# Reordering the first head's loads and keeping TensorE busy in its last waits: one decode kernel, two small edits

## The chip, the core and the metric

The kernel runs on one core of a Trainium2 chip. The metric is the device time of one execution in microseconds. A profile's span is about 2 us shorter than the timed run that it belongs to (1275.8 against 1277.7 for the kernel before). In the lines of the profile, PE is TensorE, PEld its weight loads, DVE VectorE, ACT ScalarE, POOL GpSimd, and SPq the queue that SyncE fills. The *granted clock* is the share of TensorE's full clock, here 1.00 or 0.50.

## The reference, cut to what matters

One token attends to a long cache, and a small gated block is added:

```python
xn = _layernorm(x)                                   # x: 1 x 1 x 448
q  = (xn @ wq) as 16 query heads of 256
scores = einsum(q, k_cache) * 256**-0.5              # 8 key heads, 65536 keys of 256, bf16
o  = einsum(softmax(scores), v_cache)
out = x + o @ wo + (xn + gated block of xn)          # the gated block uses w_r, w_gate, w_up, w_down
```

The key and value caches are 268 MB each, and each byte is used once. So 549 MB must be read from memory, and little else costs anything.

## The kernel before

The 65536 keys of a head are 512 columns of 128 partitions, cut into four *units* of 128 columns (8 MiB). Keys use slots 0 and 1 of an on-chip ring in turn, and values use slot 2. All loads go through one queue, in the order in which SyncE issues them. An issue waits until the slot has been read (`FREE`, `FREEH` for half of it, `VFREE`). A unit in `HALVED` is loaded as two halves with two waits.

```python
HALVED = (0, 2, 3, 4)
def k_item(u):
    need = [("FREE", u - 2)] if u >= 2 else ()
    if u >= 2 and u in HALVED:
        need = {0: [("FREEH", u - 2)], 1: need}
    slot_item("k", u, u % 2, ...two halves if u in HALVED..., need)

def v_item(t):
    slot_item("v", t, 2, None, [("VFREE", t - 1)] if t else [("QT",), ("R",), ("CONST",)])

item("wq", ...)
for u in range(U - 1):     # U = 4: key units 0, 1, 2
    k_item(u)
v_item(0)
k_item(U - 1)              # key unit 3
k_item(U)
k_item(U + 1)
for t in range(1, NT):
    v_item(t)
    ...                    # one key unit after each value unit
...                        # the last head, with other weights between
slot_item("v", NT + 3, 2, ...six pieces of LAST = [64, 32, 16, 8, 4, 4] columns..., [("SUM",)])
...                        # last rows of the output weights
```

TensorE transposes the keys (`ps_t`), multiplies them with the query (`ps_q`), and multiplies the values with the probabilities (`ps_o`). After the last value piece come a few tiny matmuls with the output weights, one copy, and the store:

```python
values(NT + 2)
values(NT + 3)             # pe_V: for each piece, wait for its load, then its matmuls
dve_ob(T); pe_oT(T)
...
for k, (i, f0, f1) in enumerate(ENDS):
    W_item("pe", ("wo_end", k))       # the last three loads of output weights
    ...                               # a pair of matmuls, 224 columns each, per block
O("dve", "RESULT", ...tensor_copy...) # then the store
```

Of the kernel before, what the change touches and what calls it, by code (L numbers as in the profile page):

```python
# [14 lines left out]
LAST = [64, 32, 16, 8, 4, 4]  # L15
DIRECT = 2
NF = 2
ACT_M = (3,)
TORD = (3, 0, 1, 2)


def bass_parallel_sum__gqa_block_cached__moe_arch_mod__decode_kernel(
# [21 lines left out]
    _, Hkv, Sk, Dh = A_k_cache.shape  # L44
# [3 lines left out]
    rep = Hq // Hkv  # L48
# [14 lines left out]
    U = NPP // SBN  # L63
    NT = U * (Hkv - 1)
# [21 lines left out]
    def S_(name, shape, dtype):  # L86
        t = nc.sbuf_tensor(name, shape, dtype)
        sb.append(t)
        return t.__enter__()
# [4 lines left out]
    slots = [ring[:, i * SLOT:(i + 1) * SLOT] for i in range(NSLOT)]  # L94
# [18 lines left out]
    p_sb = S_("p_sb", [P, HC, CH, rep], BF16)  # L113
# [25 lines left out]
    sum_f = kt_all[0:1, 3 * KB:3 * KB + 2 * D].bitcast(FP32)  # L139
    DQ = D // NF  # L140
    FROWS = 32 * (NF - 1) + 1
    res_bf = kt_all[:, 3 * KB + 2 * D:3 * KB + 2 * D + DQ]
# [17 lines left out]
    ps_tf = [t[:, :].bitcast(FP32) for t in ps_t]  # L160
# [41 lines left out]
    def put(e, kind, key, fn, sem):  # L202
        if ghost[0] and e == "pe":
            prog[e].append(("g" + kind, lab(e), key, fn, sem))
        elif not ghost[0]:
            prog[e].append((kind, lab(e), key, fn, sem))

    def W(e, *key):
        put(e, "w", key, None, None)
# [3 lines left out]
    def O(e, key, fn, sem=None, n=1):  # L213
        key = key if isinstance(key, tuple) else (key,)
        if not ghost[0]:
            weight[key] = n
        put(e, "o", key, fn, sem or e)

    def alias(e, *key, sem=None):
        put(e, "a", key, None, sem or e)  # L220
# [21 lines left out]
    def item(key, parts, need=()):  # L242
        for n in need:
            W("sp", *n)
        for ap, src, sem in parts:
            semtot[sem] = semtot.get(sem, 0) + 16
            items[key] = (sem, semtot[sem])
            prog["sp"].append(("d", here[0], ("DMA", key, len(prog["sp"])), (ap, src), sem))
# [6 lines left out]
    def slot_item(kd, u, s, parts=None, need=()):  # L255

        o = 0
        for k, (sem, J) in enumerate(parts or [("slot%d" % s, SBN)]):
            ap = slots[s][:, o * Dh:(o + J) * Dh]
            item((kd, u, k), [(ap.rearrange("p (j d) -> p j d", d=Dh), rows_src(kd, u, o, J), sem)],  # L260
                 need[k] if isinstance(need, dict) else need if k == 0 else ())
            o += J
        fed[(kd, u)] = (s, parts or [("slot%d" % s, SBN)])

    def flat_src(src, n):
        return src.rearrange("a b -> (a b)").rearrange("(p n) -> p n", p=P)
# [14 lines left out]
# [4 lines that stand above are left out]
        slot_item("k", u, u % 2, [("slot%d" % (u % 2), CH), ("half%d" % (u % 2), CH)] if u in HALVED else None, need)  # L285

    def v_item(t):
        slot_item("v", t, 2, None, [("VFREE", t - 1)] if t else [("QT",), ("R",), ("CONST",)])

    item("wq", [(wq_area, flat_src(A_wq, WQN), "wq")])  # L290
    for u in range(U - 1):
        k_item(u)
    v_item(0)
    k_item(U - 1)
    k_item(U)
    k_item(U + 1)
    for t in range(1, NT):
# [16 lines left out]
    for g, e in enumerate(("sp", "act")):  # L314
        late.append((e, g))
    items["out"] = ("out", 16 * NF)

    def W_item(e, key):
        W(e, "DMA", key)
# [97 lines left out]
    pe = nc.tensor  # L417

    def mm(*a, **k):
        return pe.matmul(*a, **k)  # L420
# [39 lines left out]
    def ev_engine(m):  # L460
        return "act" if m in ACT_M else "dve"

# [105 lines left out]
    def act_pc(t, c):  # L568
        W("act", "EXP", t // U, rep - 1)
        W("act", "PVC", t - 1, c)  # L570
        n = ((t + 1) % U) * SBN + c * CH
        O("act", ("PC", t, c), lambda it: nc.scalar.activation(out=p_sb[:, c, :, :], in_=S_sb[:, n:n + CH, :], func=ACTF.Copy), "pc")  # L572
# [14 lines left out]
    def pe_V(t, c, first, last, loose=False):  # L587
        W("pe", "PC", t, c)
        if c == 0 and first:
            W("pe", "OB", t - 1)  # L590
        s, parts = fed[("v", t)]
        e0 = 0
        for k, (_, J) in enumerate(parts):
            o0, e0 = e0, e0 + J
            lo, hi = max(o0, c * CH), min(e0, (c + 1) * CH)
            if lo >= hi:
                continue
            W_item("pe", ("v", t, k))
            direct = k > len(parts) - 1 - DIRECT and len(parts) > 1

            def f(it, lo=lo, hi=hi, direct=direct):
                kv = slots[s].rearrange("p (j d) -> p j d", d=Dh)
                if direct:
                    for j in range(lo, hi):
                        for hf in range(NH):
                            ins = mm(ps_m[0:P, C_OT + hf * rep:C_OT + (hf + 1) * rep],
                                     lhsT=kv[:, j, :].rearrange("p (d f) -> p d f", f=NH)[:, :, hf], rhs=p_sb[:, c, j - c * CH, :],
                                     start=False, stop=False, skip_group_check=True)
                    return ins
                for j in range(lo, hi, 2):  # L610
                    g = j // 2 % NG
                    ins = mm(ps_o[32 * g:32 * g + 2 * rep, :],
                             lhsT=p_sb[:, c, j - c * CH:j - c * CH + 2, :].rearrange("p n i -> p (n i)"), rhs=kv[:, j:j + 2, :],
                             start=(first and j < 2 * NG), stop=(last and j >= SBN - 2 * NG),
                             tile_position=(0, 32 * g), skip_group_check=loose)
                return ins

            O("pe", ("PV", t, c, k), f)
        alias("pe", "PVC", t, c)
        if c == HC - 1:  # L620
            alias("pe", "VFREE", t)
        if (t + 1) % U:
            act_pc(t + 1, c)
# [134 lines left out]
    def turn_K(u):  # L758
        t = u - U
        real = t >= 0  # L760
        v = max(t, 0)
        here[0] = ("B", t) if real else ("A", u)

        def ghostly(f):
            def g():
                with maybe(real):
                    f()
            return g

        at = {(2, 2): ghostly(lambda: pe_m1t(v + U - 1)), (3, 0): ghostly(lambda: pe_bc(v + U - 1)),  # L770
              (SETS - 1, 0): ghostly(lambda: pe_oT(v))}

        def block():
            pe_V(v, 0, True, True)
            pe_tot(v)
            pe_V(v, 1, True, True)
            dve_ob(v)

        k_sets(u, range(0, CSETS), at)
        bar()  # L780
        ghostly(block)()
        bar()
        k_sets(u, range(CSETS, SETS), at)

    def fin(g):
        return ps_s[32 * g:32 * g + 1, 0:DQ]

    def values(t):
        for c in range(HC):
            pe_V(t, c, t == NT, t == NU - 1, True)  # L790

    def ending():
# [32 lines left out]
        def fin_base(it):  # L825
            for g in range(NF):
                ins = mm(fin(g), lhsT=ones_f[0:1, 0:1], rhs=sum_f[:, g * DQ:(g + 1) * DQ], start=True, stop=False,
                         tile_position=(0, 32 * g), skip_group_check=True)
            return ins
# [10 lines left out]
        def fin_x(it):  # L840
            for f in range(FO // 2):
                for g in range(NF):
                    ins = mm(fin(g), lhsT=oT_h[:, FO // 2 + f, HL:HL + 1], rhs=wo_x[:, f * D + g * DQ:f * D + (g + 1) * DQ], start=False, stop=False,
# [5 lines left out]
        for k, (i, f0, f1) in enumerate(ENDS):  # L849
            W_item("pe", ("wo_end", k))  # L850

            def f(it, k=k, i=i, f0=f0, f1=f1):
                wo = wo_view(wo_end)
                for hf in range(f0, f1):
                    for g in range(NF):
                        ins = mm(fin(g), lhsT=oT_sb[:, hf, i:i + 1], rhs=wo[:, i, hf, g * DQ:(g + 1) * DQ], start=False,
# [281 lines left out]
```

## Time and profile before

| | kernel before |
|---|---|
| time | 1277.72 us, median of 3 runs (1277.71 to 1278.37) |
| span of the profiled run | 1275.8 us |
| loads in one queue | 549.03 MB, 99.7% of the span |
| TensorE busy | 75% of the span |
| last load landed (completion marks) | 1273.20 us |
| span end after that landing | 2.56 us |

Of the profile's page, the busy row of the engines and the row on the chain of waits that ended last (share of the span of each engine in it):

```profile
PE 956.0 (75%) x9735; PEld 624.7 (49%) x9735; DVE 570.3 (45%) x1078; ACT 436.2 (34%) x655; POOL 8.0 (1%) x38
DMA 80%; PE 17%; issue 1%; ACT 1%; DVE 1%; SPq 0%; ACTq 0%; DVEq 0%
```

The chain is loads for four fifths. TensorE's part is mostly work on what has just landed. The other lines that matter are in the prediction.

### The profile page before, as it was taken

The numbers are of one execution on the slowest core, as the hardware profiler recorded it, in microseconds if no ns is written. First come the engines' busy times: TensorE is split into PE (matmuls) and PEld (weight loads), VectorE is DVE, ScalarE is ACT, GpSimd is POOL, SyncE is SP. The second block draws the span as 40 slices with busy tenths as digits, with TensorE's granted clock in tenths as the row PEclk, the third lists the DMA queues.
The fourth block names the chain that finished last, engine by engine and source line by source line (L and its number), as shares of the span: only waits on it lengthen the run. The fifth ranks groups of instructions, "written<-read, shape, count | busy, mean of one in ns | idle before, by whom it ended". The sixth has DMA issues, their size and how long they took to land.

```text
span 1275.8 us, 23503 instructions
## 1 busy us (share of the span) xinstructions
PE 956.0 (75%) x9735; PEld 624.7 (49%) x9735; DVE 570.3 (45%) x1078; ACT 436.2 (34%) x655; POOL 8.0 (1%) x38
## 2 busy tenths in 40 slices
PE   3898988778777679767778776787777687677664
PEld 3676655445544455444455454454454454444321
DVE  4566554345444455343454344454444554444310
ACT  2455433244333334323333332343332333332300
POOL 2000000000000000000000000000000000000000
PEclk9899999899888899888898888898888998888886
DMA  9999999999999999999999999999999999999998
GB/s 408 426 429 443 432 436 432 434 432 438 434 429 438 427 440 429 436 436 429 438 432 436 432 434 427 440 432 434 438 427 438 432 436 434 432 432 436 426 431 353
DMA packets 12742, 549.20 MB, mean 430 GB/s; under 512 B 1335, under 2 KB 1978, under 8 KB 3386
## 3 DMA queue, kind: packets, MB, share of 16 engines
q1 hardware_dynamic: 12724, 549.03, 99.7%
q8 instruction: 8, 0.13, 0.0%
q14 instruction: 4, 0.03, 0.0%
q10 hardware_dynamic: 6, 0.00, 0.0%
HBM read 549.03 MB, written 0.00 MB: 430 GB/s over the span
## 4 chain that ended last, share of the span: by engine, by line
DMA 80%; PE 17%; issue 1%; ACT 1%; DVE 1%; SPq 0%; ACTq 0%; DVEq 0%
DMA ring<-in_A_v_cache_dram 68%; PE ps_o L420 12%; DMA ring<-in_A_k_cache_dram 7%; DMA kt_all<-in_A_wo_dram 3%; DMA ring<-in_A_wo_dram 2%; PE ps_t L420 2%; PE ps_q L420 1%; PE ps_m L420 1%; ACT kt_all L481 1%; SPq L910 0%; DVE kt_all L479 0%; ACT S_sb L562 0%; PE ps_s L420 0%; DVE kt_all L712 0%; DVE kt_all L815 0%
## 5 line engine op out<-in xcount | busy, mean ns | idle before, releaser
L420 PE MATMUL ps_t<-ident_f,ring 128*128 128x128 f32 x4096 | 586.6, 285 | 84.5 <-DMA ring<-in_A_k_cache_dram 61.6
L479 DVE COPY kt_all<-ps_t 128x1024 bf16<-128x1024 bf16 x768 | 487.0, 684 | 293.8 <-PE ps_q L420 289.0
L420 PEld LDWEIGHTS ps_t<-ident_f,ring 128*128 128x128 f32 x4096 | 450.2, 143 | 237.2 <-issue 135.2
L481 ACT ACTIVATE kt_all<-ps_t 128x1024 bf16<-128x1024 bf16 x256 | 262.0, 1023 | 508.4 <-PE ps_q L420 508.4
L420 PE MATMUL ps_o<-ring,p_sb 128*4 128x512 bf16 x2044 | 177.1, 508 | 204.6 <-DMA ring<-in_A_v_cache_dram 200.3
L420 PEld LDWEIGHTS ps_o<-ring,p_sb 128*4 128x4 bf16 x2044 | 53.0, 101 | 292.6 <-issue 264.2
L420 PE MATMUL ps_q<-kt_all,q_cur 128*2 128x512 bf16 x2056 | 164.9, 398 | 0.3 <-DVE kt_all L479 0.3
L503 ACT ACTIVATE s<-ps_q 98x512 bf16<-98x512 f32 x257 | 151.6, 590 | 1.3 <-PE ps_q L420 1.3
L585 DVE RECIPROCAL rs<-ps_m 128x4 f32<-128x4 f32 x29 | 5.3, 182 | 272.2 <-PE ps_m L420 272.2
L572 ACT ACTIVATE p_sb<-S_sb 128x128 bf16<-128x128 bf16 x64 | 18.9, 307 | 260.8 <-PE ps_o L420 260.6
L420 PEld LDWEIGHTS ps_s<-sel_bf,s 128*128 128x128 bf16 x1032 | 64.7, 98 | 5.3 <-ACT s L503 1.9
L420 PE MATMUL ps_s<-sel_bf,s 128*128 128x8 bf16 x1032 | 63.7, 167 | 1.3 <-ACT s L503 1.3
L628 DVE CAST ob_sb<-ps_o 100x512 bf16<-100x512 f32 x29 | 20.0, 691 | 89.9 <-PE ps_o L420 89.9
L420 PEld LDWEIGHTS ps_q<-kt_all,q_cur 128*2 128x2 bf16 x2056 | 26.4, 79 | 44.2 <-issue 44.2
L420 PEld LDWEIGHTS ps_m<-rowsum,ones_f 128*128 128x128 f32 x58 | 12.3, 264 | 22.6 <-issue 22.6
L481 ACT ACT_TABLE_LOAD x7 | 9.0, 1283 | 20.8 <-PE ps_q L420 20.8
L532 DVE TENSOR_REDUCE m1p<-S_sb (+1 forms) x33 | 13.9, 422 | 4.4
L420 PE MATMUL ps_m<-rowsum,ones_f 128*128 128x4 f32 x58 | 14.8, 326 | 0.0
L530 DVE CAST S_sb<-ps_s 128x256 f32 (+1 forms) x33 | 13.6, 413 | 1.9 <-PE ps_s L420 1.9
L562 ACT ACTIVATE S_sb<-S_sb,negmax 128x512 bf16<-128x512 bf16 x16 | 13.2, 851 | 3.2 <-DVE negmax L556 3.2
L420 PE MATMUL ps_m<-diag,ones_f 2*128 2x2 f32 x58 | 11.2, 260 | 3.6 <-DVE diag L547 0.6
L420 PEld LDWEIGHTS ps_m<-diag,ones_f 2*128 2x128 f32 x58 | 8.7, 187 | 10.5 <-DVE diag L547 10.5
(93 smaller groups left out, 128.3 us busy)
## 6 DMA issues: line engine op xcount, KB each, us to landing
ring<-in_A_k_cache_dram SPq DMA_DIRECT2D x8, 4096.0 KB, 30.5
ring<-in_A_v_cache_dram SPq DMA_DIRECT2D x1, 4096.0 KB, 27.3
ring<-in_A_wq_dram SPq DMA_DIRECT2D x1, 3584.0 KB, 11.5
ring<-in_A_wo_dram SPq DMA_DIRECT2D x1, 2688.0 KB, 28.7
ring<-in_A_v_cache_dram SPq DMA_DIRECT2D x1, 2048.0 KB, 31.8
ring<-in_B_w_gate_dram SPq DMA_DIRECT2D x1, 1568.0 KB, 16.5
ring<-in_B_w_up_dram SPq DMA_DIRECT2D x1, 1568.0 KB, 19.9
ring<-in_B_w_down_dram SPq DMA_DIRECT2D x1, 1568.0 KB
```

The costliest lines, as they stand in the source:

```text
L420: return pe.matmul(*a, **k)
L479: O(e, ("EV", s, m), lambda it: nc.vector.tensor_copy(out=kt[:, :], in_=tb[:, :]), f"ev{m}")
L481: O(e, ("EV", s, m), lambda it: nc.scalar.activation(out=kt[:, :], in_=tb[:, :], func=ACTF.Copy), f"ev{m}")
L503: O("act", ("EVQ", s), lambda it: nc.scalar.activation(out=s2[s % 2][0:QROWS, :], in_=ps_q[0:QROWS, :], func=ACTF.Copy), "evq")
L530: O("dve", ("SCOPY", u), lambda it: nc.vector.tensor_copy(out=S_sb[:, at(it, SBN), :], in_=ps_sn), "sc")
L532: O("dve", ("SMAX", u), lambda it: nc.vector.tensor_reduce(out=m1p[:, :, at(it, 1)], in_=S_sb[:, at(it, SBN), :].rearrange("p n i -> p i n ...
L562: O("act", ("EXP", h, i), lambda it, i=i: nc.scalar.activation(out=S_sb[:, :, i], in_=S_sb[:, :, i], func=ACTF.Exp, bias=negmax[:, i:i + 1 ...
L572: O("act", ("PC", t, c), lambda it: nc.scalar.activation(out=p_sb[:, c, :, :], in_=S_sb[:, n:n + CH, :], func=ACTF.Copy), "pc")
L585: O("dve", ("RS", t), lambda it: nc.vector.reciprocal(out=rs[:, :, :], in_=ps_m[0:P, C_TOT:C_TOT + NH * rep]))
L628: O("dve", ("OB", t), lambda it: nc.vector.tensor_copy(out=ob_sb[0:OROWS, :], in_=ps_o[0:OROWS, :]))
```

## The change

The intent is twofold. First, in the head all four key units are loaded before the first values, since the values are needed much later and TensorE waited for key unit 3. Second, nine extra matmuls, whose result nobody reads, fill TensorE's waits between the last value pieces, so that its clock stays at full speed for the final matmuls.

```diff
+WARM = {0: (5, 512), 1: (2, 512), 2: (1, 512), 3: (1, 256)}
@@ order of the loads
-    for u in range(U - 1):
+    for u in range(U):
         k_item(u)
     v_item(0)
-    k_item(U - 1)
     k_item(U)
     k_item(U + 1)
@@ pe_V, after the matmuls of piece k
             O("pe", ("PV", t, c, k), f)
+            if t == NT + 3 and k in WARM:
+
+                def keep(it, k=k):
+                    n_, cols = WARM[k]
+                    for _ in range(n_):
+                        ins = mm(ps_tf[3][0:2 * rep, 0:cols], lhsT=p_sb[:, c, 0:2, :]..., rhs=slots[0][:, 0:cols],
+                                 start=True, stop=True, skip_group_check=True)
+                    return ins
+
+                O("pe", ("WARM", k), keep)
```

More of the change, by code (lines that the diff above doesn't have):

```diff
@@ L618, in pe_V @@
             O("pe", ("PV", t, c, k), f)
+            if t == NT + 3 and k in WARM:
+                def keep(it, k=k):
+                    n_, cols = WARM[k]
+                    for _ in range(n_):
+                        ins = mm(ps_tf[3][0:2 * rep, 0:cols], lhsT=p_sb[:, c, 0:2, :].rearrange("p n i -> p (n i)"), rhs=slots[0][:, 0:cols],
+                                 start=True, stop=True, skip_group_check=True)
+                    return ins
+                O("pe", ("WARM", k), keep)
         alias("pe", "PVC", t, c)
```

## The prediction

> **What bounds the kernel now.** I read the page first, then the chain of waits in order of time, then the DMA queue's own timeline for the head, and the timelines and stretches of the last 15 us. Four units of 128 key columns make one head; a unit of keys or of values is 8 MiB (8.39 MB). A halved unit goes as two transfers of 4 MiB.
>
> The page, by slices and by queues:
>
> ```profile
> DMA  9999999999999999999999999999999999999998
> q1 hardware_dynamic: 12724, 549.03, 99.7%
> ```
>
> The transfers fill every slice but the last; one queue carries all 549 MB and occupies the 16 engines 99.7% of the span. TensorE at 75% is not the bound. To see whether the transfers ever pause, I add start and length of the DMA pieces of the chain, which gives landing times:
>
> ```profile
> 2.12 49.74 DMA ring<-in_A_k_cache_dram
> 65.07 35.30 DMA ring<-in_A_k_cache_dram
> 144.17 24.06 DMA ring<-in_A_v_cache_dram
> 172.45 34.47 DMA ring<-in_A_v_cache_dram
> 1065.05 32.00 DMA ring<-in_A_v_cache_dram
> 1103.17 32.58 DMA ring<-in_A_v_cache_dram
> ```
>
> Key unit 1 lands at 51.86, the first half of key unit 3 at 100.37, value unit 1 at 168.23, value unit 2 at 206.92; far later two value units land at 1097.05 and 1135.75. From 51.86 to 100.37 the queue moved 20 MiB (both halves of key unit 2, value unit 0, half of unit 3): 48.51 / 5 = 9.70 us per 4 MiB. From 100.37 to 168.23 it moved 28 MiB: 67.86 / 7 = 9.69. Each later pair of units takes 38.69 to 38.70 us, or 9.67 per 4 MiB, which is 433.5 GB/s. So in the head, exactly where the change reorders the queue, there is no pause now: 0.03 us per 4 MiB over twelve pieces is 0.3 us in all. Whatever the order, the same bytes must land, and the kernel's end is the last landing plus a short tail.
>
> The queue's own timeline in the head, and TensorE's one wait there:
>
> ```profile
> 48.34 0.36 SPq L910 DMA_DIRECT2D ring<-in_A_v_cache_dram  x1
> 65.07 0.33 SPq L910 DMA_DIRECT2D ring<-in_A_k_cache_dram  x1
> 76.47 0.33 SPq L910 DMA_DIRECT2D ring<-in_A_k_cache_dram  x1
> 144.17 0.33 SPq L910 DMA_DIRECT2D ring<-in_A_v_cache_dram  x1
> 100.42 1.09 PE L420 MATMUL ps_t<-ident_f,ring 128*128 128x128 f32 x8 [1.06 <-DMA ring<-in_A_k_cache_dram]
> ```
>
> These are: value unit 0 issued at 48.34, the halves of key unit 3 at 65.07 and 76.47 (each waits until TensorE has read that half's slot, key unit 1), value unit 1 at 144.17. TensorE waits 1.06 us for the first half of unit 3, because value unit 0 went ahead of it.
>
> The tail: last value pieces, two stretches with their clock, and the last steps.
>
> ```profile
> 1261.64 3.57 PE L420 MATMUL ps_o<-ring,p_sb 128*4 128x512 bf16 x32 [4.66 <-DMA ring<-in_A_v_cache_dram]
> 1266.53 1.03 PE L420 MATMUL ps_o<-ring,p_sb 128*4 128x512 bf16 x16 [1.32 <-DMA ring<-in_A_v_cache_dram]
> 1268.92 1.02 PE L420 MATMUL ps_o<-ring,p_sb 128*4 128x512 bf16 x8 [1.36 <-DMA ring<-in_A_v_cache_dram]
> 1270.21 0.60 PE L420 MATMUL ps_o<-ring,p_sb 128*4 128x512 bf16 x4 [0.26 <-DMA ring<-in_A_v_cache_dram]
> 1265.12:1268.53 3.41, 1.12 (x20) 0.32 (x16) 0.00 (x0) 0.00 (x0) 0.00 (x0) 1.00 0.99 403
> 1268.53:1271.94 3.41, 2.38 (x32) 0.88 (x32) 0.69 (x1) 0.00 (x0) 0.00 (x0) 0.50 0.92 336
> 1273.24 0.08 PEld L420 LDWEIGHTS ps_s<-kt_all,oT_sb 128*1 128x1 bf16 x2 [0.21 <-DMA kt_all<-in_A_wo_dram]
> 1273.70 0.38 DVE L862 CAST kt_all<-ps_s 33x224 bf16<-33x224 f32 x1 [1.46 <-PE ps_s L420]
> ```
>
> Each piece waits for its transfer, not for TensorE. TensorE was busy 1.12 of 3.41 us before 1268.53 and the clock then fell to 0.50, so the final matmuls run at half clock. The last piece of the output weights lets its matmuls start at 1273.24 to 1273.26; they end near 1273.65, the copy runs 1273.70 to 1274.08, and the store of the result ends the span at 1275.8.
>
> **What the Trainium skill says.** (1) "TensorE: Matmul & The Clock Gate", section "What's actually happening": the clock is half unless recent activity holds it up, judged in windows of about 3.4 us, and an idle window takes it down. The trace agrees: the clock changes only between 1.00 and 0.50, and the two stretches above are 3.41 us long. (2) Same page, "Single matmul latency": about (219 + N)/1.2 ns cold and (398 + N)/2.4 warm. For N = 224 that is 369 and 259 ns; the trace has 369 ns on average for four such matmuls (128x224) at half clock and 381 for the eight after. (3) "DMA: Bandwidth & Descriptors", section "Where 436 GB/s comes from": a ceiling of 435 GB/s. The 433.5 GB/s above sit within 0.4% of it, so the stream itself has nothing to give. (4) Same page, "Queues, rings and completion order": each engine takes descriptors in ring order. So value unit 0, issued behind both halves of key unit 3, should land behind them; the trace agrees, as unit 3, issued after value unit 0, lands 9.7 us after it.
>
> **Part 1, the order in the head.** It removes and adds no transfer; it swaps 8 MiB of values with 8 MiB of keys. Unit 2's second half lands at 51.86 + 2 x 9.70 = 71.3 in both kernels. After the change unit 3 lands in halves at 81.0 and 90.7, and value unit 0 at 110.1 instead of 90.7. The values are first read at about 138.4, so 28 us remain. TensorE loses its 1.06 us wait, starts unit 3 at about 99.2 and keeps that lead of about 1.2 us up to the first value matmuls; value unit 1 is then issued near 143.0 rather than 144.2. But its landing is fixed by the bytes ahead of it, key unit 5 landing at 168.23 - 19.36 = 148.9: it lands at 168.2 either way. Worth: 0.
>
> The one danger is that the queue now holds less. Value unit 0 cannot be issued before both waits for unit 3 are over. Unit 3's first half is issued at 65.07, 6.2 us before its predecessor lands (71.3); the second half at 76.47, 4.5 us before its predecessor lands (81.0). How much lead is needed? The first weights (3.67 MB, 8.47 us at 433.5 GB/s) took 11.5 us from issue to landing in the page's issue table, so start-up costs about 3.0 us (estimate). And value unit 1 was issued 4.7 us before 148.9 without any pause. 4.5 is enough, by some 1.5 us.
>
> **Part 2, nine matmuls.** Five of 512 columns after the first value piece, then 2 x 512, 1 x 512 and 1 x 256, each in a wait. At full clock a 512-column matmul streams in 512/2.4 = 213 ns, at half clock 427 (estimates; page as in (2)). The waits are 1.32, 1.36, 0.26 and (to 1270.89, where the fifth piece starts) 0.08 us; the last two grow by some 0.2 to 0.5 us once the third and fourth piece themselves run at full clock. At full clock the fillers take 1.07, 0.43, 0.21 and 0.11 us, and fit. At half clock the first five take 2.13 us, 0.8 too long, but the third piece starts only at 1268.92, with 1.4 us to take it up. So they delay nothing that ends the kernel.
>
> What they buy: busy time before 1268.53 rises from 1.12 to about 2.6 of 3.41 us, so the clock should stay up there. In the next stretch the same work at full clock plus fillers comes to 2.2 to 2.3 us by my estimate, 65%. Cutting the whole trace into such 3.41 us stretches, those at full clock with 50% or more busy nearly always kept it, those under 42% nearly always lost it. I take 75% that the final matmuls run at full clock. The only ones on the path are the pair after the last landing: 0.39 us, to become 0.26. Saving 0.13 us; the copy and the store are on other engines. Expected: 0.75 x 0.13 = 0.1 us.
>
> **Sum.** 1277.72 - 0 - 0.1 = 1277.6 us.
>
> **Rivals.** (a) *The removed wait of 1.06 us passes to the end*: 1276.6. For it: the wait is on TensorE's own path into the first values. Against: value landings stand 38.70 us apart throughout, and TensorE waits for values in every later turn, so its lead ends in a longer wait. (b) *The thinner queue runs dry* between the halves of unit 3: each us of pause is a us at the end, since nothing later has room to catch up. The half clock at unit 1's start (half until 56.8) may last up to 1.9 us longer in another run, costing up to 1 us of lead; still 3.5 against 3.0. If it happens, +0.3 to +1 us: 1277.9 to 1278.6. I give it 10%. (c) *A filler stands in the way*, if the clock is low throughout: the fourth piece would start some 0.2 us late and its copy too, at most +0.3 us. (d) *The clock still falls* before the last pair: 1277.7, no change. (e) TensorE becomes the bound: at 75% busy with 2 us more idle it does not.
>
> **Range and chances.** All rivals lie within 1.2 us of the prediction. The three runs before spread over 0.66 us, more than the whole effect. I take 1276.9 to 1278.4. Two per cent is 25.6 us, twenty times any term here: within 2% 0.99, the rest split evenly.
>
> **What would show it.** Right: value unit 0 issued just after 76.5 and TensorE's wait of 1.06 us near 100.4 gone; value unit 1 landing still near 168.2 and units 38.70 us apart; clock 1.00 over the last three microseconds, the last pair of 224 columns about 260 ns, and the copy at 1273.57 instead of 1273.70. Wrong: a landing of value unit 1 later than 168.5 (rival b) or earlier than 167.5 (rival a); any value piece whose wait before it names a filler matmul; a time outside 1276.9 to 1278.4.

## The result and the profile after

| | before | after |
|---|---|---|
| median | 1277.72 us | 1279.11 us |
| all runs | 1277.72, 1278.37, 1277.71, 1278.06, 1277.18, 1277.64 | 1278.76, 1279.09, 1279.38, 1279.53, 1279.12, 1277.22 |

A ratio in this text is the mean time of one kernel's runs over that of the other's runs of the same rounds, so it isn't quite the ratio of the medians quoted. Here it is 1.0008, with a 95% interval of 0.9995 to 1.0021. By the 2% mark that is as predicted. But the median lies 1.4 us higher and outside the predicted range, and the runs fall in two groups: five from 1278.76 up, one at 1277.22. The profiled run is the one of 1278.76.

The page of the changed kernel, the main queue and the chain:

```profile
q1 hardware_dynamic: 12724, 549.03, 99.6%
DMA 78%; PE 18%; ACT 2%; issue 1%; DVE 1%; SPq 1%; ACTq 0%; DVEq 0%
```

The bytes and packets are the same, and the queue's share went from 99.7 to 99.6%. A tenth of a per cent of the span is 1.3 us, so this rounded figure can only hint. The queue's timeline in the head (start, length, engine, line):

```profile
65.52 0.33 SPq L920 DMA_DIRECT2D ring<-in_A_k_cache_dram  x1
76.94 0.33 SPq L920 DMA_DIRECT2D ring<-in_A_k_cache_dram  x1
77.39 0.35 SPq L920 DMA_DIRECT2D ring<-in_A_v_cache_dram  x1
142.06 0.33 SPq L920 DMA_DIRECT2D ring<-in_A_v_cache_dram  x1
```

Both halves of key unit 3 now go first, at 65.52 and 76.94, and value unit 0 follows 0.45 us later. Before, value unit 0 had been in the queue from 48.34 on. TensorE at the start of key unit 3:

```profile
99.99 1.06 PE L420 MATMUL ps_t<-ident_f,ring 128*128 128x128 f32 x8 [0.18 <-ACT kt_all L481]
```

The wait of 1.06 us for the load is gone; what is left is 0.18 us, for ScalarE. The chain of waits, whose DMA pieces give a landing as start plus length:

```profile
2.12 49.70 DMA ring<-in_A_k_cache_dram
142.06 26.36 DMA ring<-in_A_v_cache_dram
172.64 34.48 DMA ring<-in_A_v_cache_dram
...
1183.87 29.52 DMA ring<-in_A_wo_dram
```

Key unit 1 lands at 51.82 (51.86 before), value unit 1 at 168.42 (168.23), value unit 2 at 207.12 (206.92, so still 38.70 apart), and the output weights near the end at 1213.39. In the kernel before the last is:

```profile
1183.30 29.61 DMA ring<-in_A_wo_dram
```

That is 1212.91. So the kernel is 0.19 us late after the first head and 0.48 us late at 1213. The rest comes in the last stretch. To see it I took from the trace the completion marks of every transfer: sixteen of them, one for each DMA engine, and a transfer counts as landed at the last. Landing times in us, the after kernel's delay in brackets:

```
transfer                        before     after
key unit 2, second half          71.30     71.30
key unit 5                      148.87    149.07  (+0.20)
value unit 1                    168.23    168.42  (+0.19)
output weights, second part    1212.91   1213.39  (+0.48)
second last full value unit    1232.26   1232.74  (+0.48)
last full value unit           1251.77   1252.08  (+0.31)
first piece of the last unit   1261.51   1262.58  (+1.07)
last load of all               1273.20   1274.25  (+1.05)
```

The span ends 2.56 us after the last landing in the one and 2.55 in the other. **The whole difference is a later landing of the same bytes**: 0.2 us in the head, 0.3 near 1213 (half of it made up again), and 0.76 in the first piece of the last unit.

The tail of the changed kernel. First TensorE's last pieces, one group of fillers and the final matmuls; then two windows with the busy times of the engines and, as the last three figures, granted clock, DMA share and GB/s; then VectorE's copy:

```profile
1262.71 3.54 PE L420 MATMUL ps_o<-ring,p_sb 128*4 128x512 bf16 x32 [5.10 <-DMA ring<-in_A_v_cache_dram]
1266.08 1.25 PE L420 MATMUL ps_t<-ring,p_sb 128*4 128x512 bf16 x5
1267.61 1.03 PE L420 MATMUL ps_o<-ring,p_sb 128*4 128x512 bf16 x16 [0.28 <-DMA ring<-in_A_v_cache_dram]
1270.00 0.60 PE L420 MATMUL ps_o<-ring,p_sb 128*4 128x512 bf16 x8 [0.94 <-DMA ring<-in_A_v_cache_dram]
1271.29 0.39 PE L420 MATMUL ps_o<-ring,p_sb 128*4 128x512 bf16 x4 [0.48 <-DMA ring<-in_A_v_cache_dram]
1273.80 0.91 PE L420 MATMUL ps_s<-kt_all,oT_sb 128*1 128x224 bf16 x8
```

```profile
1266.08:1269.50 3.42, 2.70 (x27) 0.84 (x22) 0.00 (x0) 0.00 (x0) 0.00 (x0) 1.00 0.99 395
1269.50:1272.91 3.41, 1.98 (x34) 0.88 (x34) 0.69 (x1) 0.00 (x0) 0.00 (x0) 1.00 0.73 265
```

```profile
1274.75 0.38 DVE L872 CAST kt_all<-ps_s 33x224 bf16<-33x224 f32 x1 [1.52 <-PE ps_s L420]
```

Each piece still waits for its load, so no filler stands in the way. The clock is full for two windows instead of one, but falls at 1272.91, before the last eight matmuls (from 1273.80 on), of which the last pair ends the chain. So in this run the fillers bought nothing.

### The profile page after: what moved, and what is told of

It is laid out like the page before. It is cut to its first block, busy times and chain, and to the rows that moved or that the text cites. A ratio compares the mean times of both kernels' runs of the same rounds, so it can differ in the third digit from the quotient of the medians.

```text
span 1276.8 us, 23521 instructions
## 1 busy us (share of the span) xinstructions
PE 951.4 (75%) x9744; PEld 623.2 (49%) x9744; DVE 570.0 (45%) x1078; ACT 436.6 (34%) x655; POOL 8.1 (1%) x38
## 3 DMA queue, kind: packets, MB, share of 16 engines
q1 hardware_dynamic: 12724, 549.03, 99.6%
## 4 chain that ended last, share of the span: by engine, by line
DMA 78%; PE 18%; ACT 2%; issue 1%; DVE 1%; SPq 1%; ACTq 0%; DVEq 0%
DMA ring<-in_A_v_cache_dram 69%; PE ps_o L420 12%; DMA ring<-in_A_k_cache_dram 4%; PE ps_t L420 3%; DMA kt_all<-in_A_wo_dram 3%; DMA ring<-in_A_wo_dram 2%; ACT kt_all L481 2%; PE ps_q L420 2%; PE ps_m L420 1%; SPq L920 1%; DVE kt_all L479 0%; ACT S_sb L562 0%; PE ps_s L420 0%; DVE kt_all L722 0%; DVE kt_all L825 0%
## 5 line engine op out<-in xcount | busy, mean ns | idle before, releaser
L420 PE MATMUL ps_o<-ring,p_sb 128*4 128x512 bf16 x2044 | 172.3, 497 | 207.5 <-DMA ring<-in_A_v_cache_dram 203.1
```

Source lines behind the costliest of these rows:

```text
L420: return pe.matmul(*a, **k)
```

## The experiments

**Theories.** (Q) *The thin queue*: the second half of key unit 3 is issued too late in some runs, and DMA engines run dry for a moment. (F) *The fillers*: the nine matmuls cost time, by what they do in the tail or by lengthening the program. (C) *Chance*: the same kernels on another chip would show no difference.

Three theories, fifteen runs. I call **lead** the time from the issue of the second half of key unit 3 to the landing of the transfer that is ahead of it in the queue. In the changed kernel that is the first half of key unit 3.

### Each part alone, and the whole again (e1, e2, e3, e4: one chip)

e1 has only the order of the head, e2 only the fillers, e3 is the changed kernel itself. e4 is the changed kernel with key unit 1 in halves as well, so that TensorE enters that unit earlier and the issue comes earlier:

```diff
 e1: -    for u in range(U - 1):     +    for u in range(U):      (and  -    k_item(U - 1))
 e2: +WARM = {...}                   and the block in pe_V, nothing else
 e4: the whole change, and
-    HALVED = (0, 2, 3, 4)
+    HALVED = (0, 1, 2, 3, 4)
-    items[("k", 1, 1)] = ("half1", 16)
```

> Only the new order in the head, no filler matmuls. Theory A (the thinner queue ran dry between the halves of key unit 3, and the engines that were ahead lost their lead): as slow as the whole change, about 1279.1 us, with the second half of unit 3 landing 9.9 us after the first and the landing times of the 16 engines bunched after it. Theory B (the fillers or their extra instructions cost it): like the kernel before, 1277.7.

> Only the nine filler matmuls, old order in the head. Theory A: like the kernel before or 0.1 us under it, 1277.5 to 1277.8. Theory B: about 1279.1 us. Theory C (the two add up, each about half): 1278.4.

> The changed kernel itself on this chip, as the measure for the others: 1279.1 us if the loss is its own, 1277.7 if the earlier 1.4 us was the chip or chance.

> The whole change, and key unit 1 loaded in two halves as well, so that TensorE starts it earlier and the halves of unit 3 are issued some 4 to 6 us sooner: second half about 9 us instead of 4.1 us before its predecessor lands. Theory A: the pause goes, about 1277.6 us. Theory B: stays near 1279.1.

| run | times, us | median | ratio to before, 95% |
|---|---|---|---|
| before, nine runs | 1277.21 to 1278.67 | 1277.54 | |
| e1 | 1277.51 1277.38 1277.47 1277.42 1277.31 | 1277.42 | 0.9998, 0.9984 to 1.0011 |
| e2 | 1277.20 1277.12 1277.39 1277.64 1278.27 | 1277.39 | 0.9999, 0.9986 to 1.0013 |
| e3 | 1277.34 1279.70 1277.44 1279.21 1277.97 | 1277.97 | 1.0007, 0.9993 to 1.0021 |
| e4 | 1277.51 1277.41 1277.52 1277.56 1277.33 | 1277.51 | 0.9998, 0.9985 to 1.0012 |

Neither part alone showed anything. The whole again had slow runs (1279.70 and 1279.21) and quick ones in turn, so the effect is a matter of single runs, not of a fixed cost. e4, with a lead of 6.06 us in its profile (issue at 74.93, landing at 80.99), had no slow run. (The edit gained less than the expected 4 to 6 us: the issue comes 2.0 us earlier than in the profile after, 1.05 us earlier than in e3.) This speaks for Q over F, as e4 has all fillers. But with e1 all quick, Q was not yet safe: order alone should have had slow runs as well.

### Taking lead away and giving it back (e5 to e8: a second chip)

e5 repeats e1. e6 and e7 are e1 with a later issue of the second half: it waits in addition for a group of transposes of key unit 2, the second group in e6 and the fourth in e7 (their order is 3, 0, 1, 2). e8 is the whole change, but value unit 0 is put *between* the halves of key unit 3, so that the queue is never thin:

```diff
 e6 (order alone, and)
+            if u == U - 1:
+                need[1] = list(need[1]) + [("T", 2 * SETS, 0)]       # e7: 2 instead of 0
 e8 (whole change, and)
+            if (kd, u, k) == ("k", U - 1, 1):
+                v_item(0)
-    v_item(0)
```

> Only the new order in the head, five more runs. In the whole change 7 of 11 runs took 1278.7 us or more, here none of 5 so far. Theory A (a pause in the head that depends on how early the second half of unit 3 is issued, which moves with the clock's phase; no filler needed): about half of the runs at 1278.5 to 1279.7. Theory B2 (the slow runs need the fillers too): again all within 1277.2 to 1277.7.

> New order, no fillers, the second half of unit 3 issued 1.3 us later on purpose, so some 3.2 us before its predecessor lands, less than in any run seen. Theory A: a pause in every run, unit 3's second half lands 10.5 to 11.2 us after the first instead of 9.71, and every run is at 1278.3 us or more. Theory B2: 1277.4.

> New order, no fillers, second half of unit 3 issued 2.9 us later, so some 1.6 us before its predecessor lands. Any theory in which bytes bound the kernel: the slowest engine loses 2.5 to 3 us there, the 16 landing times bunch up, and the end is 2 to 4 us later, 1279.5 to 1281.5. If it stays under 1278.2 a pause in the head is not carried to the end.

> The whole change with fillers, but value unit 0 issued between the two halves of key unit 3, so that the queue never holds less than 8 MiB there. Theory A: no pause, all runs 1277.3 to 1277.7. Theory B2 (fillers cost it): slow runs of 1278.7 or more remain.

| run | times, us | median | ratio to before, 95% |
|---|---|---|---|
| before, nine runs | 1277.54 to 1278.60 | 1277.76 | |
| e5 | 1277.66 1277.73 1277.88 1278.13 1278.08 | 1277.88 | 1.0000, 0.9987 to 1.0014 |
| e6 | 1278.59 1279.24 1279.78 1278.24 1279.38 | 1279.24 | 1.0010, 0.9996 to 1.0024 |
| e7 | 1279.11 1279.85 1279.17 1280.40 1279.40 | 1279.40 | 1.0014, 1.0000 to 1.0028 |
| e8 | 1277.35 1277.51 1277.39 1277.99 1277.27 | 1277.39 | 0.9997, 0.9984 to 1.0011 |

e5 met neither expectation: its five runs, up to 1278.13, were neither half of them slow nor all within 1277.7.

The issue and landing of the second half, first in e6, then in e7 (duration and start of the issue, then us from issue to landing):

```profile
L911 SPq DMA_DIRECT2D ring<-in_A_k_cache_dram x1: 328/328/328, 77.4 to 77.4; - x1
DMA to landing us min/median/max: 14.8/14.8/14.8
```

```profile
L911 SPq DMA_DIRECT2D ring<-in_A_k_cache_dram x1: 328/328/328, 78.8 to 78.8; - x1
DMA to landing us min/median/max: 14.0/14.0/14.0
```

So the half lands at 92.2 and 92.8. Its predecessor landed at 81.07 and 80.88, by the marks, and 4 MiB takes 9.71 us when nothing pauses. e6 lost 1.42 us with a lead of 3.70, and e7 lost 2.18 us with a lead of 2.07. **Without a single filler, a shorter lead makes every one of ten runs late (1278.24 or more).** Of the 42 runs of the kernel before, six took that long. And e8, with all fillers, was late in none. The delay is shown to come from the lead; F as the sole cause is refuted, and so is C: on this one chip, no run of e6 and e7 was as quick as the slowest of e5 and e8 (1278.13). The sizes were surprising: three of e7's five runs took less than the 1279.5 us that I had expected at least, and e7 had 1.63 us less lead than e6 but ended only 0.16 us later in the median. The pause in the head is not simply handed on to the end.

### Nine matmuls in another place (e9, e10, e11: a third chip)

Could a longer program alone make slow runs more frequent? e9 is the order alone with nine matmuls before the last unit, where TensorE has time. e10 is the changed kernel, e11 the order alone again.

```diff
 e9 (order alone, and)  between values(NT + 2) and values(NT + 3):
+        def pad(it):
+            for cols in 8 * [512] + [256]:
+                ins = mm(ps_tf[3][0:2 * rep, 0:cols], lhsT=zero_bf[:, 0:2 * rep], rhs=slots[0][:, 0:cols], start=True, stop=True, ...)
+            return ins
+        O("pe", "PAD", pad)
```

> New order in the head, and nine such matmuls (8 x 512 and 256 columns) in the long idle stretch before the last value unit instead of in its waits: same number of instructions as the whole change. If more instructions of TensorE make the difference between the order alone (10 of 10 runs under 1278.2) and the whole change (7 of 11 at 1278.7 or more): several runs over 1278.5. If only the place of the fillers in the last waits does it: 1277.3 to 1278.1. If only the lead counts (theory A), the same mix as the other two of this call.

> The changed kernel a third time, with the two below on one chip. Theory A (lead of the second half of unit 3 decides, and it varies with the clock's phase by run): a spread from 1277.3 to 1279.7, the profiled run slow if its lead is under 4.2 us and fast if it is over 4.5.

> Order alone, same chip. Theory A: some runs over 1278.5 as in the whole change, the profiled run slow if its lead is under 4.2 us. Theory B2 (needs the fillers as well): again all under 1278.2.

| run | times, us | median | ratio to before, 95% |
|---|---|---|---|
| before, nine runs | 1277.49 to 1278.53 | 1277.60 | |
| e9 | 1277.75 1278.76 1278.16 1277.52 1278.28 | 1278.16 | 1.0003, 0.9990 to 1.0017 |
| e10 | 1277.86 1279.51 1277.31 1277.85 1277.42 | 1277.85 | 1.0002, 0.9988 to 1.0016 |
| e11 | 1277.50 1277.64 1277.58 1279.51 1278.01 | 1277.64 | 1.0003, 0.9990 to 1.0017 |

e11 gives what e1 and e5 had not: order alone, no filler, a run of 1279.51. So the slow runs belong to the order. The three kernels aren't told apart here, and this batch is inconclusive on whether the fillers make slow runs more frequent.

### The edge of the lead, and looks at the changed kernel (e12 to e15: the first chip)

What was still open: how much lead is needed, and whether a slow run of the unchanged change has the short lead. e12 has the edit of e6 with `("T", 2 * SETS, 3)`, the first group of all, and so delays the issue least. e13, e14 and e15 are the changed kernel, one profiled run each, without an edit.

> New order, no fillers, second half of unit 3 issued about 0.8 us later (after one group of unit 2's transposes), so 3.0 to 4.4 us before its predecessor lands. Theory A: between the plain order (3 of 20 runs over 1278.2) and the 1.3 us delay (5 of 5 over 1278.2): most runs over 1278.2, and a pause at the second half (9.8 to 10.8 us instead of 9.71) if the profiled lead is under 4.2 us.

> One profile of the changed kernel. Theory A: if the lead of the second half of unit 3 is under 4.2 us, that half lands more than 9.8 us after the first and the run takes over 1278.2; if over 4.5 us, 9.71 us and under 1278.2. A slow run with a lead over 4.5 us would speak against it.

> As the look before: lead under 4.2 us with a slow run, over 4.5 us with a fast one.

> As the look before: lead under 4.2 us with a slow run, over 4.5 us with a fast one.

e12 ran at 1278.65, 1279.42, 1278.31, 1279.21 and 1279.41 (median 1279.21; before 1277.73 on nine runs; ratio 1.0009, 0.9995 to 1.0022). e13 took 1279.63, e14 1277.49 and e15 1277.59. One of the nine runs of the kernel before took 1279.18 in this batch, the only such run of it. It wasn't profiled, and its cause is open.

e13 and e14 are the same program, a slow and a quick run of it. In each, first a stretch of TensorE's work on key unit 1 with its clock, then the second half of key unit 3. The slow run, e13:

```profile
54.90:57.90 3.00, 3.00 (x21) 2.94 (x18) 2.07 (x3) 1.60 (x3) 0.00 (x0) 0.50 1.01 437
```

```profile
L920 SPq DMA_DIRECT2D ring<-in_A_k_cache_dram x1: 327/327/327, 77.1 to 77.1; - x1
DMA to landing us min/median/max: 14.4/14.4/14.4
```

The quick run, e14:

```profile
54.90:57.90 3.00, 2.95 (x33) 2.20 (x30) 1.89 (x3) 1.60 (x3) 0.00 (x0) 0.98 0.96 415
```

```profile
L920 SPq DMA_DIRECT2D ring<-in_A_k_cache_dram x1: 328/328/328, 76.0 to 76.0; - x1
DMA to landing us min/median/max: 14.9/14.9/14.9
```

TensorE enters key unit 1 at half clock in both, after a wait of some 4 us, at 52.04 and 52.08. In e14 the clock rises at 55.03, in e13 only at 58.04. Over these three microseconds e14 gets through 33 matmuls and e13 through 21. The half of the slot that the second half of unit 3 needs is read 1.17 us later, and the lead is 3.95 instead of 5.16 us. The half lands 10.50 us after its predecessor in e13 and 9.71 in e14.

All profiled runs together, from the completion marks and the issues. The column *mean* is what the sixteen engines lost there on average: how much further than the 9.71 us of an undisturbed half the mean of their marks moved from the first half to the second. It does not depend on which mark is whose:

```
       half clock  second half  lead   second half  mean   value unit 1  last load  run
       until       issued              lands after         lands         lands      took
e7     55.53       78.81        2.07   11.89        1.35   170.25        1274.60    1279.11
e6     55.42       77.37        3.70   11.13        0.79   169.65        1274.05    1278.59
e13    58.04       77.15        3.95   10.50        0.76   169.08        1275.12    1279.63
after  57.76       76.94        4.07    9.94        0.35   168.42        1274.25    1278.76
e12    56.40       76.81        4.19    9.78        0.46   168.95        1274.14    1278.65
e5     56.82       76.45        4.44    9.71        0.11   168.08        1273.15    1277.66
e10    56.91       76.62        4.47    9.71        0.27   168.29        1273.34    1277.86
e1     56.38       76.34        4.60    9.71        0.24   168.12        1273.00    1277.51
e9     55.40       76.00        5.08    9.71        0.05   168.26        1273.24    1277.75
e11    55.41       75.75        5.12    9.72        0.03   168.08        1272.96    1277.50
e3     55.03       75.98        5.15    9.71        0.04   168.31        1272.99    1277.34
e14    55.03       75.98        5.16    9.71        0.06   168.33        1273.14    1277.49
e15    55.83       76.00        5.18    9.72        0.05   168.37        1273.23    1277.59
e4     55.79       74.93        6.06    9.71        0.00   168.16        1272.97    1277.51
```

For the landing the dividing line is sharp. In the five profiles with a lead of 4.19 us or less the half lands late and the run takes 1278.59 us or more. In the nine with 4.44 us or more it lands on time, and no run is above 1277.86. But on time isn't unhurt: the mean shows that the sixteen engines together already lose time at 4.60 us of lead (0.24 us each on average), hardly any above 5 us, and none at 6.06. In e8 and in the kernel before there is no such lead to speak of (in e8 the predecessor lands 24.5 us after the issue, at 100.46).

Over all runs: the changed kernel and the order alone, with or without matmuls elsewhere, took 1278.7 us or more, the mark that I call slow here, in 11 of 39 runs. The kernels without the thin spot or with more lead (before, e2, e4, e8) did so in 1 of 57. The delayed ones (e6, e7, e12) did so in 11 of 15, and none of those 15 was below 1278.24.

### Where the time is lost later

The pause of the profiled run after is 0.23 us, yet the end is 1.05 us late. The marks of that run show why this can be. Here are the marks of the sixteen engines at the first half of key unit 3 and at the second half, in us before the last engine, sorted:

```
first half,  81.01:  1.73 1.61 1.56 1.54 1.52 1.50 1.49 1.49 1.14 1.09 0.75 0.30 0.29 0.20 0.10 0
second half, 90.95:  1.76 1.67 1.55 1.47 1.42 1.33 1.15 0.98 0.92 0.53 0.51 0.44 0.35 0.24 0.09 0
```

The engines do not run in step. Each keeps its distance to the last for many transfers, and the quickest finish 1.7 us early. The quickest therefore run dry first. What they lose doesn't show in the landing, which waits for the slowest, but it eats the slack that they had. Besides the loads, the page lists a few transfers of another kind, instruction fetches by their name. On queue 8 it is eight, 0.13 MB in all and so 16 KB each:

```profile
q8 instruction: 8, 0.13, 0.0%
```

By the trace each takes about 1.0 us; the last two start at 1237.44 and 1258.14 in this run. Around the last one the marks jump. In the kernel before, one of four marks around 2.2 us ahead of the last disappears and one at 0.76 appears; nothing is delayed. In the run after, one of two marks near 0.75 us disappears, a new last mark appears, and the piece lands 10.50 us after the one ahead of it instead of 9.74. In e13 there is such a jump after the fetch of 1204.69: a transfer of output weights lands 2.96 us after the one ahead of it instead of 1.39. e12 has the plainest case, in the head itself: its half was only 0.07 us late, but value unit 1 landed 0.72 us later than in the kernel before. Nearly all of that comes in one step, around a fetch of 8 KB at 125.49 on another queue: there a key half lands 10.39 us after the one ahead of it, the last mark moves back by 0.68 us and the other fifteen keep their places. In the kernel before, the fetch at 127.61 leaves that step at 9.71. So I read it thus: a fetch sets one engine back, which costs nothing if that engine has slack, and in the slow runs it had lost it in the head. This is argued from marks that don't name their engine; it isn't shown.

### The clock in the tail, over all profiles

Nine profiles have the fillers. In the kernel before, and in e1, full clock lasts one window of 3.41 us in the tail. With the fillers it lasts two windows in all nine. It then fell each time, after a second window that was 1.65 to 2.36 us busy of 3.41 (48 to 69%). The last windows of e14, then its last matmuls and its copy:

```profile
1266.76:1270.18 3.42, 2.46 (x33) 0.84 (x26) 0.00 (x0) 0.00 (x0) 0.00 (x0) 1.00 1.00 387
1270.18:1273.59 3.41, 2.35 (x37) 1.07 (x37) 0.96 (x3) 0.00 (x0) 0.00 (x0) 1.00 0.45 162
```

```profile
1272.69 0.75 PE L420 MATMUL ps_s<-kt_all,oT_sb 128*1 128x224 bf16 x8 [0.30 <-DMA kt_all<-in_A_wo_dram]
...
1273.49 0.38 DVE L872 CAST kt_all<-ps_s 33x224 bf16<-33x224 f32 x1 [1.36 <-PE ps_s L420]
```

Here the second window ends at 1273.59, after the last pair. Each matmul of the pair takes 257 ns, and the copy starts 0.35 us after the last landing. In the profile after, the window ends at 1272.91, before the pair. The pair takes 391 and 394 ns, and the copy starts 0.50 us after the last landing. The second window outlasts the pair in e2, e3, e14 and e15, and not in after, e4, e8, e10 and e13. It saves 0.16 us where it does: the span ends 2.40 instead of 2.56 us after the last landing.

## Why the prediction was right or wrong

- **The bound**: right. In every profile the end is the last landing plus 2.40 to 2.58 us.
- **The new order is worth nothing by itself**: right where the lead suffices. Value unit 1 lands at 168.08 to 168.37 in those profiles, against 168.23 before, and TensorE's wait of 1.06 us is gone (it starts unit 3 at 99.99 rather than 99.2, in part since its half clock lasted until 57.76 instead of 56.80; e5, with 56.82, starts it at 99.50). Rival (a), the wait passing to the end, is refuted: the quickest of all runs of the new order took 1277.22.
- **The failed step is "4.5 is enough, by some 1.5 us".** The mechanism was named, as rival (b), and so was its trigger: the half clock at the start of unit 1 "may last up to 1.9 us longer in another run". It ended between 55.03 and 58.04, against 56.80 in the profile that I read. What was mis-sized is the lead that is needed. I took 3.0 us from a landing, which is the last engine's. The runs put the edge between 4.19 and 4.44 us. The marks suggest why: the quickest engines are done 1.7 to 2.1 us before the landing from which I counted, and they start to wait that much sooner. So the margin was about 0.1 to 0.3 us instead of 1.5, well within the 1.0 us by which I let the clock move it. For the quick engines there was no margin at all, as the column *mean* shows. My second proof had the same fault: value unit 1, issued 4.7 us ahead in the kernel before, did land on time, but the mean of its marks moved by 19.43 us instead of 19.35. The 10% follows from that error: 11 of 39 runs of that order were slow, and 8 of the 16 timed runs of the changed kernel. That the median missed the range is partly chance: five of the first six runs were slow, while the later medians of the same kernel, 1277.97 and 1277.85, lie inside it.
- **"Each us of pause is a us at the end"**: wrong in both directions. The pause and the lateness of the end, against the kernel before, were 0.23 and 1.05 us in the profile after, 0.79 and 1.92 in e13, 1.42 and 0.85 in e6, 2.18 and 1.40 in e7. So the upper end of rival (b), 1278.6, was also too low: slow runs took 1278.8 to 1279.7.
- **My own test would have missed it.** "A landing of value unit 1 later than 168.5" was to show rival (b). It landed at 168.42 in a slow run. The landing is the slowest engine's; the harm was in the others' slack.
- **The fillers**: no value piece was delayed enough to move the end, so rival (c) did not come true. In four profiles (e2, e3, e14, e15) the first fillers ran at half clock and the fifth ran among the matmuls of the second piece, but the third piece waited for its load again, as I had expected. The saving of 0.13 us measured 0.16. But 75% was too high. Windows with 48 to 69% busy lost the clock in nine of nine, so "50% or more busy nearly always kept it" failed in the tail. Over the whole trace before, the rule does come out: of 246 full-clock windows with 50% or more busy 245 kept the clock, of 43 under 42% none did. What sets the windows of the tail apart was not tested. Whether the pair is still warm depends on where the window ends: 4 of 9 profiles. The worth is then about 4/9 x 0.16 = 0.07 us, which no series of five runs shows.
- **Open**: whether the fillers make slow runs more frequent. Order alone, e9 included, was slow in 2 of 20 timed runs, the whole change in 8 of 16. But five of the eight come from the first session, which had no run of the order alone. In the sessions with both it is 0 of 5 against 2 of 5, and 2 of 10 against 1 of 5. That the order is slow without them is shown by e11 and by e6, e7 and e12. A reason for a higher rate with them was not found. Open too is which engine each fetch hits.

The version with the best median against its own chip's kernel before is e8 (1277.39 against 1277.76): the removed wait doesn't return, the queue stays full, the fillers are in. Its ratio of 0.9997 with an interval from 0.9984 to 1.0011 is not told apart from 1. No version clearly beats the kernel before; e8 only takes the harm out.

## What to carry to other kernels

Where one queue of loads is the bound, an order that issues a transfer later, behind a wait on another engine, is only as good as its lead in the worst run: count the lead from the first DMA engine that runs dry, not from the landing, and subtract what the clock's phase can take from the engine that frees the buffer. When a change can only gain tenths of a microsecond, put something long that needs no wait (here the values, as in e8) ahead of the transfer that does, and look at several runs, since one profile shows one phase. A landing that is on time doesn't prove that nothing was lost.

## What the Trainium skill lacked or had wrong

- "DMA: Bandwidth & Descriptors", section "Specifications", gives about 0.6 us to the first byte for a transfer issued by SyncE. It has nothing on how early a transfer must be queued for a stream not to pause. Here a half unit landed late when it was issued 4.19 us or less before the landing of the transfer ahead, and on time with 4.44 us or more; at 4.60 us the engines still lost 0.24 us on average.
- No page that I found says that a transfer's sixteen engines may keep a fixed distance from each other: 1.7 to 2.1 us between the first and the last mark, held over many transfers in a row.
- "Runtime: NRT & Kernel Launch", section "Instruction fetch mechanics", has fetches in blocks of 16 KiB and calls their cost mostly hidden. Neither it nor any page that I found gives what they cost a stream of loads. Here there were eight of 16 KB, each about 1.0 us. In the run after, the first piece of the last unit, around one of them, took 10.50 instead of 9.74 us.
- "TensorE: Matmul & The Clock Gate", section "What's actually happening", has the clock fall after an idle window of about 3.4 us. Here it fell after windows with 1.65 to 2.36 us of matmuls in 3.41, in nine of nine profiles. It does say that the windows run free of the kernel, and the spread of the clock's rise over 55.03 to 58.04 us agrees.
